# The first microseconds of a causal convolution and gated feed-forward kernel: softmax of the taps on eight partitions, the last band's products on ScalarE, and the first rows of x through SyncE's queue

## The chip, the cores and the metric

The kernel runs on one core of a Trainium2 chip. The core has TensorE (PE; matmuls, and PEld for its weight loads), VectorE (DVE), ScalarE (ACT), GpSimd (POOL) and SyncE (SP), each with its own instruction stream, and sixteen DMA engines which serve the transfers that SP, ACT and POOL issue. The metric is the device time of one execution in microseconds. Before the change three runs took 515.96, 516.28 and 517.74 us, with a median of 516.28 us.

## What is computed

The input x has 8 sequences of 3904 rows with 192 columns in fp32. The 192 columns belong to 8 heads of 24. For each head, a softmax over 7 weights gives 7 taps, and every row becomes the sum of itself and its six predecessors, weighted with the taps (a causal depthwise convolution, zero-padded at the start of a sequence). The 31232 resulting rows go through a gated feed-forward block.

```python
w = np.exp(weight - weight.max(-1, keepdims=True))
w = w / (w.sum(-1, keepdims=True) + 1e-09)          # 8 heads x 7 taps
x_pad = np.concatenate([np.zeros((B, 6, D)), x], axis=1)
out = np.einsum('hk,bskhg->bshg', w, x_unf)         # x_unf: rows s .. s+6 of x_pad, by heads
x = out.reshape(B * S, D)
a, b = x @ w1, x @ w2                               # 192 -> 1024
h = a * b @ w3                                      # 1024 -> 1024
return h @ w_out                                    # 1024 -> 192
```

## The kernel before

The tokens are split into two streams (NS = 2) of 15616 rows, r = 0 and r = 1. Partitions 0 to 63 hold stream 0 and partitions 64 to 127 stream 1, and a 64-row matmul works on one of them. w3 and w_out are multiplied with one another at the start (lines 550 to 570), so that in the steady part each round of 512 tokens per stream is two products: first_product (line 510; w1 and w2, cast by ScalarE, gated by VectorE) and second_product (line 520).

The convolution of the first batches is a matmul too. A window of x has 64 rows (Q), 58 of them new (ST) and 6 the predecessors (PAD). For each head a 64x64 "band" matrix holds the taps on its diagonals. conv (line 381) multiplies windows with bands, pe_transpose and joint_transposes (lines 445 and 596) turn the result for the products. Batches of windows are loaded by load_x(b) (line 112), from fp32 in memory to bf16 on the chip, on POOL's queue.

Instructions are in the program's order on every engine, and an engine waits at the head of its own stream. What happens in the first 16 us, in the order of the code:

- wall, the 8x7 weights, is loaded to one partition on ACT's queue (lines 143 and 144). VectorE sets constants (lines 157 to 163). ScalarE loads its table and does a first exponential (line 164).
- wfirst, the first quarter of w1 and w2 in fp32, is loaded by two DMAs on SP's queue (line 171).
- POOL issues load_x0(0), makes both halves of diag (line 183), issues load_x0(1), then two DMAs for the first window's 58 rows of each stream (line 189; the six rows before them are zeros, line 160), then load_x(1), load_w(1) (the second quarter of w1 and w2, already as bf16), casts one half of wfirst (cast_w(1, 1, ...), line 193), then load_w(2), load_x(2), and copies and loads on (lines 203 to 208).
- TensorE multiplies zeros for a while (warm(6), line 217).
- The softmax runs on one partition, 56 elements (lines 223 to 231): maximum, difference, exponential on ScalarE, sum, reciprocal, product. Two matmuls with the row `half` (line 237) spread the taps over 128 partitions, and they end in wsb.
- band(g, e) (line 252) makes c, the products of diag shifted by 7 taps with wsb, on VectorE, and 28 matmuls which add them up in PSUM; put (line 578) moves the result to Aband. There are four bands. ScalarE moves the first two, VectorE the other two, and ScalarE casts wfirst between and after them (lines 582 to 589).
- conv(0, 0, 4) and conv(0, 4, 4) follow (lines 622 and 623), three transposes, conv(1, 0, H), the first parts of the first product and, in the middle of the product of round 0 (line 652), conv(2, 0, 4) and conv(2, 4, 4), which read what load_x(2) brought.

There are four pairs of PSUM banks (banks and drained, lines 78 to 87); each step takes one pair and gives it back when its result has been moved.

Of the kernel before, what the change touches and what calls it, by code (L numbers as in the profile page):

```python
# [16 lines left out]
def kernel(  # L17
# [17 lines left out]
    PAD = K - 1  # L35

    NS = 2
    TS = B * S // NS
# [4 lines left out]
    Q = 64  # L43
    ST = Q - PAD
# [22 lines left out]
    const = ctx.enter_context(tc.tile_pool(name="const", bufs=1))  # L67
# [17 lines left out]
    def drained(p):  # L85
        assert p not in free
        free.append(p)
# [17 lines left out]
    x_rows = x.rearrange("b s d -> (b s) d")  # L105
    xb_of, zero_rows = {}, {}

    def x_spans(r, i, m):
        return bass.AP(tensor=x.tensor, offset=(r * TS + tok(i) - PAD) * D,
                       ap=[[D, Q], [ST * D, m], [1, D]])  # L110
# [29 lines left out]
            else:  # L140
                tiles.append((xb, 0))

    wall = const.tile([1, H, K], FP32)
    nc.scalar.dma_start(out=wall, in_=weight.rearrange("(o h) k -> o h k", o=1))
# [9 lines left out]
    half = const.tile([1, 3 * Q], BF16)  # L154
# [4 lines left out]
    nc.vector.memset(ones, 1.0)  # L159
    nc.vector.memset(xb0[:, 0, :], 0.0)  # L160
    nc.vector.memset(half, 0.0)
    nc.vector.memset(half[:, Q:2 * Q], 1.0)
    nc.vector.memset(ident, 0.0)
    nc.scalar.activation(out=tiny, in_=tiny, func=ACT.Exp)

    WC = (0, DFF // 4, DFF // 2, DFF * 3 // 4, DFF)
    wd = [const.tile([128, NP, DFF], BF16, name=f"wd{i}", tag=f"wd{i}") for i in range(2)]
    w_rows = [w.rearrange("(k q) f -> q k f", q=Q) for w in (moe_w1, moe_w2)]

    for i in range(2):  # L170
        nc.sync.dma_start(out=wfirst[:, i], in_=w_rows[i][:, :, 0:WC[1]])

    def load_w(part):
        cs = slice(WC[part], WC[part + 1])
        for i in range(2):
            nc.gpsimd.dma_start(out=wd[i][0:Q, :, cs], in_=w_rows[i][:, :, cs])  # L176

    def load_x0(r):
        nc.gpsimd.dma_start(out=xb0[Q * r:Q * r + Q, 1:, :], in_=x_spans(r, 1, 2 * n0 - 1))  # L179

    load_x0(0)
    for p0 in (0, Q):
        nc.gpsimd.affine_select(  # L183
            out=diag[p0:p0 + Q], in_=ones[p0:p0 + Q].to_broadcast([Q, Q + PAD]),
            pattern=[[-1, Q + PAD]], compare_op=ALU.is_equal, fill=0.0, base=0,
            channel_multiplier=1)
    load_x0(1)
    for r in range(NS):
        nc.gpsimd.dma_start(out=xb0[Q * r + PAD:Q * r + Q, 0, :],  # L189
                            in_=x_rows[r * TS:r * TS + ST, :])  # L190
    load_x(1)
    def cast_w(i, r, f):
        f(out=wd[i][Q * r:Q * r + Q, :, 0:WC[1]], in_=wfirst[:, i])  # L193
# [16 lines left out]
    def warm(n):  # L210
        p, t = banks()
        for j in range(n):
            nc.tensor.matmul(t[:, j % 2, :], zeros, zeros[:, 0:1].to_broadcast([128, CH]),
                             start=True, stop=True)
        drained(p)

    warm(6)

    wmax = const.tile([1, H], FP32)
    wsum = const.tile([1, H], FP32)  # L220
    wrow = const.tile([1, H, K], BF16)
    wsb = const.tile([128, 2, 2, K], BF16)
    nc.vector.reduce_max(out=wmax, in_=wall, axis=AX.X)
    nc.vector.tensor_tensor(
        out=wall, in0=wall, in1=wmax.unsqueeze(2).to_broadcast([1, H, K]), op=ALU.subtract)
    nc.scalar.activation(out=wall, in_=wall, func=ACT.Exp)
# [8 lines left out]
    wrow = wrow.rearrange("p (g e a) k -> p g e a k", g=2, a=2)  # L235
# [9 lines left out]
    def band_of(h, r):  # L245
# [3 lines left out]
    taps = bass.AP(tensor=d0.tensor, offset=d0.offset,  # L249
                   ap=[list(d0.ap[0]), [1, K], [1, Q]])  # L250

    def band(g, e):
        c = slot([128, K, Q], BF16, "cprod")
        nc.vector.tensor_tensor(
            out=c, in0=taps, in1=wsb[:, g, e].unsqueeze(2).to_broadcast([128, K, Q]),
            op=ALU.mult)
        p, bps = banks()
        for k in range(K):
            for v in range(2):
                for r in range(2):  # L260
                    rs = slice(Q * r, Q * r + Q)
                    o = Q * (r ^ v)
                    nc.tensor.matmul(bps[o:o + Q, v, 0:Q], ident[rs, rs], c[rs, k, :],
                                     start=(k == 0), stop=(k == K - 1))
        return p, Aband[:, g, e], bps[:, :, 0:Q]
# [115 lines left out]
    def conv(b, h0, nh, evict=None):  # L381
        n = SIZES[b] // 2
        if h0 == 0:
            tag, bufs = ("alone", 1) if GRID <= b else ("convo", 2)
            convo_of[b] = work.tile([128, n, NP, NS, Q], BF16, tag=tag, bufs=bufs, name="convo")
        convo = convo_of[b]
        p, cps = banks()
        wd = nh * G

        def view(ps, r):  # L390
            return cps[ps, r, 0:n * wd].rearrange("p (w g) -> p w g", g=wd)

        for j in range(nh):
            h = h0 + j
            for c in range(2):
                xb, w0 = xb_of[b][c]
                for r in range(NS):
                    nc.tensor.matmul(  # L398
                        view(slice(Q * c, Q * c + Q), r)[:, :, j * G:(j + 1) * G],
                        band_of(h, r),  # L400
                        xb[Q * r:Q * r + Q, w0:w0 + n, h * G:(h + 1) * G],
                        start=True, stop=True)
# [170 lines left out]
    V, A, P = nc.vector.tensor_copy, nc.scalar.copy, nc.gpsimd.tensor_copy  # L573
# [4 lines left out]
    def put(f, p, dst, src):  # L578
        f(out=dst, in_=src)
        drained(p)  # L580

    cast_w(0, 0, A)
    put(A, *band(0, 0))
    put(A, *band(0, 1))
    cast_w(0, 1, A)
    made = [band(1, 0), band(1, 1)]
    put(V, *made[0])
    put(V, *made[1])
    cast_w(1, 0, A)

    def move_all(p, moves, fs):
        for f, m in zip(fs, moves):
            move(f, m)
        drained(p)
# [92 lines left out]
    def put_rows(b, last):  # L687
# [7 lines left out]
        out=wv, in0=wv, in1=top.unsqueeze(2).to_broadcast([128, H, K]), op=ALU.subtract)  # L695
# [5 lines left out]
        out=wv, in0=wv, in1=top.unsqueeze(2).to_broadcast([128, H, K]), op=ALU.mult)  # L701
# [84 lines left out]
```

## Time and profile before

| | |
|---|---|
| median of three runs | 516.28 us |
| profiled execution | 517.34 us |
| its span, first to last instruction | 515.6 us |
| TensorE busy in the span | 508.2 us |
| VectorE busy | 401.9 us |
| ScalarE busy | 351.3 us |
| GpSimd busy | 321.4 us |
| granted TensorE clock | 1.000 |

All lines come from one profiled execution. A line of the timeline has the start in us from the beginning of the span, the length in us, the engine, the line of the code, the operation, the names out<-in, the shape, the number of instructions put together, and in brackets the idle time of the engine ahead of it with what ended that. An engine with a q behind its name (SPq, ACTq) is the issue of a DMA, not its transfer. A line of the waits has who waited for whom, us in total, times and the longest. In a group of instructions, the numbers behind the bar are busy us, mean ns of one, and the idle time before them; for one source line the numbers are the shortest, the median and the longest in ns, then the first and last start. In the DMA views q0 is the queue of the DMAs that POOL issues, q1 that of SP; a row has packets, MB, and the time that the packets took as a share of what sixteen DMA engines have in the window. Shares can exceed 100% since packets overlap on an engine. The windows rows have the length, the busy time of PE, PEld, DVE, ACT and POOL with the number of instructions, the granted clock, the DMA share and GB/s.

### The profile page before, as it was taken

The numbers are of one execution on the slowest core, as the hardware profiler recorded it, in microseconds if no ns is written. First come the engines' busy times: TensorE is split into PE (matmuls) and PEld (weight loads), VectorE is DVE, ScalarE is ACT, GpSimd is POOL, SyncE is SP. The second block draws the span as 40 slices with busy tenths as digits, with TensorE's granted clock in tenths as the row PEclk, the third lists the DMA queues.
The fourth block names the chain that finished last, engine by engine and source line by source line (L and its number), as shares of the span: only waits on it lengthen the run. The fifth ranks groups of instructions, "written<-read, shape, count | busy, mean of one in ns | idle before, by whom it ended". The sixth has DMA issues, their size and how long they took to land.

```text
span 515.6 us, 13632 instructions
## 1 busy us (share of the span) xinstructions
PE 508.2 (99%) x5608; PEld 338.9 (66%) x5608; DVE 401.9 (78%) x475; ACT 351.3 (68%) x466; POOL 321.4 (62%) x447
## 2 busy tenths in 40 slices
PE   8899999999999999999999999999999999999997
PEld 4444698555894558944589444884449855498577
DVE  6679723889958999589995999949999499972970
ACT  6787644777657776577765777657776577744762
POOL 8510624279999999899983999749997491000000
PEclk9999999999999999999999999999999999999999
DMA  9989999993984984787827798278932851025004
GB/s 119 165 153 123 145 194 204 195 208 80 134 251 130 131 104 101 241 156 100 103 83 240 147 106 98 93 239 140 108 46 93 247 122 32 1 99 174 7 3 154
DMA packets 137410, 67.91 MB, mean 132 GB/s; under 512 B 98899, under 2 KB 135939, under 8 KB 137283
## 3 DMA queue, kind: packets, MB, share of 16 engines
q0 software_dynamic: 48096, 26.92, 37.0%
q1 hardware_dynamic: 89105, 40.01, 33.5%
q8 instruction: 44, 0.72, 0.5%
q14 instruction: 19, 0.16, 0.1%
q10 hardware_dynamic: 146, 0.10, 0.1%
HBM read 39.60 MB, written 36.56 MB: 148 GB/s over the span
## 4 chain that ended last, share of the span: by engine, by line
PE 93%; DMA 3%; POOL 2%; ACT 1%; DVE 1%; issue 0%; POOLq 0%; ACTq 0%
PE pairs L481 58%; PE pairs L532 32%; PE pairs L398 2%; DMA xT<-rows 2%; DMA xb<-in_x_dram 1%; PE pairs L567 1%; ACT asb L489 1%; POOL wd L176 0%; DVE abT L500 0%; POOL xb L126 0%; PE pairs L606 0%; POOL xb L179 0%; POOL xb L189 0%; POOL wd L193 0%; POOL diag L183 0%
## 5 line engine op out<-in xcount | busy, mean ns | idle before, releaser
L500 DVE TENSOR_TENSOR abT<-asb,pairs 128x1024 bf16<-128x1024 bf16 (+1 forms) x245 | 298.0, 1217 | 70.1 <-ACT asb L489 53.6
L481 PE MATMUL pairs<-xT,wd 64*128 64x512 bf16 (+3 forms) x3000 | 319.7, 371 | 1.2 <-DMA xT<-rows 0.6
L489 ACT CAST asb<-pairs 128x1024 bf16<-128x1024 f32 (+1 forms) x245 | 247.1, 1009 | 68.1 <-PE pairs L481 68.0
L481 PEld LDWEIGHTS <-wd 64*128 64x128 bf16 x3000 | 160.2, 94 | 154.4 <-issue 2.9
L532 PE MATMUL pairs<-W_sb,abT 128*128 128x192 bf16 x1952 | 165.0, 246 | 0.0
L532 PEld LDWEIGHTS <-abT 128*128 128x128 bf16 x1952 | 159.9, 98 | 5.3 <-issue 5.1
L537 ACT COPY osb<-pairs 128x384 f32<-128x384 f32 x122 | 58.6, 480 | 83.3 <-PE pairs L532 82.6
L331 POOL TENSOR_TENSOR acc<-acc,term 128x384 f32<-128x384 f32 (+1 forms) x120 | 107.4, 895 | 9.4
L328 POOL TENSOR_TENSOR term<-xv,wv 128x384 f32<-128x384 bf16 (+1 forms) x144 | 107.6, 747 | 0.0
L317 DVE SCALAR_TENSOR_TENSOR pairs<-xv,wv,pairs 128x384 f32<-128x384 bf16 (+1 forms) x120 | 68.7, 572 | 7.2 <-ACT pairs L315 3.4
L364 POOL DMA_DIRECT2D rows<-y x6 | 3.7, 614 | 68.8 <-DVE y L320 59.9
L334 POOL TENSOR_TENSOR y<-acc,term 128x192 bf16<-128x192 f32 (+5 forms) x60 | 26.5, 467 | 1.9
L419 ACT CAST convo<-pairs 128x864 bf16<-128x864 f32 (+9 forms) x49 | 26.6, 615 | 1.6 <-PE pairs L398 1.5
L325 POOL TENSOR_TENSOR acc<-xv,wv 128x384 f32<-128x384 bf16 (+1 forms) x24 | 18.3, 763 | 12.5 <-DMA xv<-in_x_dram 12.4
L419 DVE CAST convo<-pairs 128x960 bf16<-128x960 f32 (+4 forms) x10 | 8.2, 858 | 17.2 <-PE pairs L398 17.2
L320 DVE SCALAR_TENSOR_TENSOR y<-xv,wv,pairs 128x192 bf16<-128x192 bf16 (+5 forms) x60 | 18.0, 351 | 1.1
L126 POOL DMA_DIRECT2D xb<-in_x_dram x20 | 13.9, 719 | 4.2 <-DMA xb<-in_x_dram 3.0
L342 POOL DMA_DIRECT2D xb<-in_x_dram x20 | 15.1, 772 | 0.0
L544 POOL DMA_DIRECT2D out_dram<-osb x8 | 6.1, 763 | 14.1 <-ACT osb L537 11.1
L398 PE MATMUL pairs<-xb,Aband 64*64 64x216 bf16 (+6 forms) x416 | 12.5, 238 | 1.5 <-DMA xb<-in_x_dram 1.4
L279 POOL DMA_DIRECT2D xv<-in_x_dram x12 | 13.0, 1088 | 0.0
L315 ACT ACTIVATE pairs<-xv,wv 128x384 f32<-128x384 bf16 (+1 forms) x24 | 12.8, 549 | 0.0
(65 smaller groups left out, 75.3 us busy)
## 6 DMA issues: line engine op xcount, KB each, us to landing
out_dram<-osb SPq DMA_DIRECT2D x52, 384.0 KB
xv<-in_x_dram POOLq DMA_DIRECT2D x10, 672.0 KB, 9.8
xb<-in_x_dram POOLq DMA_DIRECT2D x20, 216.0 KB, 7.8
rows<-y POOLq DMA_DIRECT2D x5, 768.0 KB, 5.5
out_dram<-osb POOLq DMA_DIRECT2D x8, 384.0 KB, 5.7
w3rows<-in_moe_w_dram POOLq DMA_DIRECT2D x2, 1024.0 KB, 11.8
xb<-in_x_dram POOLq DMA_DIRECT2D x8, 240.0 KB, 7.2
rows<-convo SPq DMA_DIRECT2D x6, 288.0 KB
```

Of the source, the lines that this page charges most:

```text
L317: f.scalar_tensor_tensor(out=flat, in0=xs(k), scalar=tap(k), in1=flat, op0=ALU.mult, op1=ALU.add)
L325: f.tensor_tensor(out=flat, in0=xs(PAD), in1=wide(PAD), op=ALU.mult)
L328: f.tensor_tensor(out=term.rearrange("p (m g) -> p m g", g=G), in0=xs(k), in1=wide(k), op=ALU.mult)
L331: f.tensor_tensor(out=acc, in0=acc, in1=term, op=ALU.add)
L334: f.tensor_tensor(out=dst, in0=by_row[:, :, r, cs], in1=term[:, :, r, cs], op=ALU.add)
L398: nc.tensor.matmul(view(slice(Q * c, Q * c + Q), r)[:, :, j * G:(j + 1) * G], band_of(h, r), xb[Q * r:Q * r + Q, w0:w0 + n, h * G:(h + 1) ...
L419: f[e % len(f)](out=dst, in_=part)
L481: nc.tensor.matmul(p[:, r, e * n:e * n + n], wd[i][rs, k, ft * 128:(ft + 1) * 128], xT[k][rs, r0 + c0:r0 + c1], start=(k == 0), stop=(k == ...
L489: nc.scalar.copy(out=asb, in_=pa)
L500: nc.vector.tensor_tensor(out=dst, in0=asb, in1=pb, op=ALU.mult)
L532: nc.tensor.matmul(ops[:, (g - g0) * D:(g - g0) * D + D], ab[:, jt, r, g * 128:(g + 1) * 128], W_sb[:, jt, :], start=(jt == 0), stop=(jt = ...
L537: f(out=osb[:, g0:g0 + per, :].rearrange("p g d -> p (g d)"), in_=ops[:, 0:per * D])
```

## The change

The weights are loaded to eight partitions, one head each, on SP's queue ahead of wfirst. The softmax is done with one head per partition: a negated maximum, an exponential with this maximum as bias, a sum, a reciprocal, and one instruction that multiplies with the reciprocal and with diag, so that each head's taps stand in its own block of columns and are zeros elsewhere. Two matmuls with a block of ones (8x64) spread them to the two halves of the partitions. The two copies of diag to ident go from VectorE to ScalarE. warm(6) becomes warm(5).

The bands are made in the order (0, 0), (0, 1), (1, 1), (1, 0). The products of (1, 1) are made by ScalarE, seven instructions of 128x64 with the taps from a copy wlast in fp32. VectorE moves the first two results, ScalarE the other two.

The 58 rows per stream of the first window are loaded as fp32 to a tile xfirst by two DMAs on SP's queue behind wfirst, and no longer by POOL to bf16. ScalarE casts them to xb0[:, 0, :] ahead of conv(0, ...). The second half of diag is made after load_x0(1). POOL casts both of wfirst's parts for partitions 64 to 127. ScalarE casts the parts for partitions 0 to 63 in halves: columns 0 to 127 of w1 ahead of conv(0, ...)'s evictions, those of w2 behind them, the rest after the three transposes.

```diff
-    wall = const.tile([1, H, K], FP32)
-    nc.scalar.dma_start(out=wall, in_=weight.rearrange("(o h) k -> o h k", o=1))
+    wall = const.tile([H, K], FP32)
+    nc.sync.dma_start(out=wall, in_=weight)
...
+    ones_h = const.tile([H, Q], BF16)
+    xfirst = const.tile([128, D], FP32)
...
-    nc.vector.memset(xb0[:, 0, :], 0.0)
-    nc.vector.memset(half, 0.0)
-    nc.vector.memset(half[:, Q:2 * Q], 1.0)
+    nc.vector.memset(xfirst, 0.0)
+    nc.vector.memset(ones_h, 1.0)
...
     for i in range(2):
         nc.sync.dma_start(out=wfirst[:, i], in_=w_rows[i][:, :, 0:WC[1]])
+    for r in range(NS):
+        nc.sync.dma_start(out=xfirst[Q * r + PAD:Q * r + Q, :],
+                          in_=x_rows[r * TS:r * TS + ST, :])
...
     load_x0(0)
-    for p0 in (0, Q):
...
+    diagonal(0)
     load_x0(1)
-    for r in range(NS):
-        nc.gpsimd.dma_start(out=xb0[Q * r + PAD:Q * r + Q, 0, :],
-                            in_=x_rows[r * TS:r * TS + ST, :])
+    diagonal(Q)
     load_x(1)
-    def cast_w(i, r, f):
-        f(out=wd[i][Q * r:Q * r + Q, :, 0:WC[1]], in_=wfirst[:, i])
+    def cast_w(i, r, f, c0=0, c1=WC[1]):
+        f(out=wd[i][Q * r:Q * r + Q, :, c0:c1], in_=wfirst[:, i, :, c0:c1])
...
     load_w(1)
-    cast_w(1, 1, nc.gpsimd.tensor_copy)
+    for i in range(2):
+        cast_w(i, 1, nc.gpsimd.tensor_copy)
...
-    warm(6)
+    warm(5)
...
-    wrow = const.tile([1, H, K], BF16)
+    wrow = const.tile([H, 2, 2, 2, K], BF16)
     wsb = const.tile([128, 2, 2, K], BF16)
-    nc.vector.reduce_max(out=wmax, in_=wall, axis=AX.X)
-    nc.vector.tensor_tensor(
-        out=wall, in0=wall, in1=wmax.unsqueeze(2).to_broadcast([1, H, K]), op=ALU.subtract)
-    nc.scalar.activation(out=wall, in_=wall, func=ACT.Exp)
-    nc.vector.tensor_copy(out=ident[0:Q, 0:Q], in_=diag[0:Q, 0:Q])
+    wlast = const.tile([128, K], FP32)
+    nc.vector.tensor_reduce(out=wmax, in_=wall, axis=AX.X, op=ALU.max, negate=True)
+    nc.scalar.activation(out=wall, in_=wall, func=ACT.Exp, bias=wmax)
+    nc.scalar.copy(out=ident[0:Q, 0:Q], in_=diag[0:Q, 0:Q])
     nc.vector.reduce_sum(out=wsum, in_=wall, axis=AX.X)
     nc.vector.reciprocal(out=wsum, in_=wsum)
-    nc.vector.tensor_tensor(
-        out=wrow, in0=wall, in1=wsum.unsqueeze(2).to_broadcast([1, H, K]), op=ALU.mult)
-    nc.vector.tensor_copy(out=ident[Q:128, Q:128], in_=diag[Q:128, 0:Q])
+    nc.vector.scalar_tensor_tensor(
+        out=wrow.rearrange("h g e a k -> h (g e a) k"),
+        in0=wall.unsqueeze(1).to_broadcast([H, H, K]), scalar=wsum,
+        in1=diag[0:H, 0:H].unsqueeze(2).to_broadcast([H, H, K]), op0=ALU.mult, op1=ALU.mult)
+    nc.scalar.copy(out=ident[Q:128, Q:128], in_=diag[Q:128, 0:Q])
...
     for a in range(2):
-        nc.tensor.matmul(wbc, half[:, Q - Q * a:Q - Q * a + 128], wrow[:, :, :, a],
-                         start=(a == 0), stop=(a == 1))
+        nc.tensor.matmul(wbc[Q * a:Q * a + Q], ones_h, wrow[:, :, :, a], start=True, stop=True)
     nc.vector.tensor_copy(out=wsb, in_=wbc)
+    nc.scalar.copy(out=wlast, in_=wbc[:, 1, 1])
...
         c = slot([128, K, Q], BF16, "cprod")
-        nc.vector.tensor_tensor(
-            out=c, in0=taps, in1=wsb[:, g, e].unsqueeze(2).to_broadcast([128, K, Q]),
-            op=ALU.mult)
+        if (g, e) == (1, 1):
+            for k in range(K):
+                nc.scalar.activation(out=c[:, k], in_=diag[:, k:k + Q], func=ACT.Copy,
+                                     scale=wlast[:, k:k + 1])
+        else:
+            nc.vector.tensor_tensor(
...
-    cast_w(0, 0, A)
-    put(A, *band(0, 0))
-    put(A, *band(0, 1))
-    cast_w(0, 1, A)
-    made = [band(1, 0), band(1, 1)]
-    put(V, *made[0])
-    put(V, *made[1])
-    cast_w(1, 0, A)
+    made = [band(0, 0), band(0, 1), band(1, 1), band(1, 0)]
+    for f, b in zip((V, V, A, A), made):
+        put(f, *b)
+    A(out=xb0[:, 0, :], in_=xfirst)
+    cast_w(0, 0, A, 0, 128)
...
     move_all(*conv(0, 4, 4, ()), (A, A))
+    cast_w(1, 0, A, 0, 128)
     for k, f in enumerate((V, V, A)):
...
         drained(p)
+    for i in range(2):
+        cast_w(i, 0, A, 128)
     move_all(*conv(1, 0, H, "streams"), (A, V))
```

More of the change, by code (lines that the diff above doesn't have):

```diff
@@ L153 @@
     zeros = const.tile([128, 128], BF16)
-    half = const.tile([1, 3 * Q], BF16)
+    ones_h = const.tile([H, Q], BF16)
+    xfirst = const.tile([128, D], FP32)
     ident = const.tile([128, 128], BF16)
@@ L179, in load_x0, with diagonal @@
         nc.gpsimd.dma_start(out=xb0[Q * r:Q * r + Q, 1:, :], in_=x_spans(r, 1, 2 * n0 - 1))
-    load_x0(0)
-    for p0 in (0, Q):
+    def diagonal(p0):
         nc.gpsimd.affine_select(
@@ L186 @@
             channel_multiplier=1)
+    load_x0(0)
+    diagonal(0)
     load_x0(1)
-    for r in range(NS):
-        nc.gpsimd.dma_start(out=xb0[Q * r + PAD:Q * r + Q, 0, :],
-                            in_=x_rows[r * TS:r * TS + ST, :])
+    diagonal(Q)
     load_x(1)
-    def cast_w(i, r, f):
-        f(out=wd[i][Q * r:Q * r + Q, :, 0:WC[1]], in_=wfirst[:, i])
+    def cast_w(i, r, f, c0=0, c1=WC[1]):
+        f(out=wd[i][Q * r:Q * r + Q, :, c0:c1], in_=wfirst[:, i, :, c0:c1])
     def copy_w(part, i, f):
@@ L215, in warm @@
         drained(p)
-    warm(6)
-    wmax = const.tile([1, H], FP32)
-    wsum = const.tile([1, H], FP32)
-    wrow = const.tile([1, H, K], BF16)
+    warm(5)
+    wmax = const.tile([H, 1], FP32)
+    wsum = const.tile([H, 1], FP32)
+    wrow = const.tile([H, 2, 2, 2, K], BF16)
     wsb = const.tile([128, 2, 2, K], BF16)
-    nc.vector.reduce_max(out=wmax, in_=wall, axis=AX.X)
-    nc.vector.tensor_tensor(
-        out=wall, in0=wall, in1=wmax.unsqueeze(2).to_broadcast([1, H, K]), op=ALU.subtract)
-    nc.scalar.activation(out=wall, in_=wall, func=ACT.Exp)
-    nc.vector.tensor_copy(out=ident[0:Q, 0:Q], in_=diag[0:Q, 0:Q])
+    wlast = const.tile([128, K], FP32)
+    nc.vector.tensor_reduce(out=wmax, in_=wall, axis=AX.X, op=ALU.max, negate=True)
+    nc.scalar.activation(out=wall, in_=wall, func=ACT.Exp, bias=wmax)
+    nc.scalar.copy(out=ident[0:Q, 0:Q], in_=diag[0:Q, 0:Q])
     nc.vector.reduce_sum(out=wsum, in_=wall, axis=AX.X)
     nc.vector.reciprocal(out=wsum, in_=wsum)
-    nc.vector.tensor_tensor(
-        out=wrow, in0=wall, in1=wsum.unsqueeze(2).to_broadcast([1, H, K]), op=ALU.mult)
-    nc.vector.tensor_copy(out=ident[Q:128, Q:128], in_=diag[Q:128, 0:Q])
+    nc.vector.scalar_tensor_tensor(
[3 more added lines that the diff above has]
+    nc.scalar.copy(out=ident[Q:128, Q:128], in_=diag[Q:128, 0:Q])
     pw, wbc = banks()
     wbc = wbc[:, 0, 0:H * K // 2].rearrange("p (g e k) -> p g e k", g=2, e=2)
-    wrow = wrow.rearrange("p (g e a) k -> p g e a k", g=2, a=2)
     for a in range(2):
-        nc.tensor.matmul(wbc, half[:, Q - Q * a:Q - Q * a + 128], wrow[:, :, :, a],
-                         start=(a == 0), stop=(a == 1))
+        nc.tensor.matmul(wbc[Q * a:Q * a + Q], ones_h, wrow[:, :, :, a], start=True, stop=True)
     nc.vector.tensor_copy(out=wsb, in_=wbc)
+    nc.scalar.copy(out=wlast, in_=wbc[:, 1, 1])
     drained(pw)
@@ L253, in band @@
         c = slot([128, K, Q], BF16, "cprod")
-        nc.vector.tensor_tensor(
-            out=c, in0=taps, in1=wsb[:, g, e].unsqueeze(2).to_broadcast([128, K, Q]),
-            op=ALU.mult)
+        if (g, e) == (1, 1):
[4 more added lines that the diff above has]
+            nc.vector.tensor_tensor(
+                out=c, in0=taps, in1=wsb[:, g, e].unsqueeze(2).to_broadcast([128, K, Q]),
+                op=ALU.mult)
         p, bps = banks()
```

## The prediction

> **What bounds the kernel now.** I read the page first, then TensorE's waits over the whole span, then the chain of waits and the timeline of the first 22 us.
>
> ```profile
> span 515.6 us, 13632 instructions
> PE 508.2 (99%) x5608; PEld 338.9 (66%) x5608; DVE 401.9 (78%) x475; ACT 351.3 (68%) x466; POOL 321.4 (62%) x447
> ```
>
> TensorE is busy in all but 7.4 us, so anything that moves its first dense stretch moves the end by as much. Its waits, longest first:
>
> ```profile
> PE pairs L398 <- DMA xb<-in_x_dram: 1.4, 1, 1.4
> PE pairs L213 <- DVE ones L159: 1.1, 1, 1.1
> PE pairs L481 <- DMA xT<-rows: 0.6, 1, 0.6
> ```
>
> The largest lies in the stretch that the change edits. The chain shows what ends it, and the timeline what TensorE does on both sides:
>
> ```profile
> 9.21 0.70 POOL xb L126
> 9.91 5.97 DMA xb<-in_x_dram
> ...
> 15.92 0.36 PE pairs L398 x15
> ```
>
> ```profile
> 0.81 0.51 ACTq L144 DMA_DIRECT2D wall<-in_weight_dram  x1
> 0.82 1.41 SPq L171 DMA_DIRECT2D wfirst<-in_moe_w_dram  x2
> ...
> 1.07 2.74 PE L213 MATMUL pairs<-zeros 128*128 128x512 bf16 x6 [1.07 <-DVE ones L159]
> ...
> 1.35 1.28 ACT L164 ACT_TABLE_LOAD   x1 [1.35 <-PEq L770]
> ...
> 2.11 0.20 DVE L223 TENSOR_REDUCE wmax<-wall 1x8 f32<-1x56 f32 x1 [0.62 <-DMA wall<-in_weight_dram]
> ...
> 2.76 0.23 ACT L226 ACTIVATE wall<-wall 1x56 f32<-1x56 f32 x1
> ...
> 3.52 1.10 POOL L189 DMA_DIRECT2D xb<-in_x_dram  x2
> ...
> 4.24 2.23 DVE L254 TENSOR_TENSOR cprod<-diag,wsb 128x448 bf16<-128x448 bf16 x4
> 4.47 0.83 ACT L193 CAST wd<-wfirst 64x768 bf16<-64x768 f32 x1 [1.49 <-DMA wfirst<-in_moe_w_dram]
> ...
> 4.91 2.20 PE L263 MATMUL pairs<-cprod,ident 64*64 64x64 bf16 x112
> 5.55 0.27 ACT L579 CAST Aband<-pairs 128x128 bf16<-128x128 f32 x1 [0.24 <-PE pairs L263]
> ...
> 6.90 0.86 PE L398 MATMUL pairs<-xb,Aband 64*64 64x72 bf16 x32
> ...
> 7.17 0.82 POOL L193 CAST wd<-wfirst 64x768 bf16<-64x768 f32 x1
> ...
> 14.33 0.23 PE L398 MATMUL pairs<-xb,Aband 64*64 64x96 bf16 x1
> ...
> 15.92 0.36 PE L398 MATMUL pairs<-xb,Aband 64*64 64x96 bf16 x15 [1.36 <-DMA xb<-in_x_dram]
> 16.21 1.47 PE L481 MATMUL pairs<-xT,wd 64*128 64x512 bf16 x12
> ```
>
> Read it as a race of two runners to 15.92, where conv(2, ...) goes on. One is TensorE's own front: bands, the first convolution at 6.90, transposes, first products, at conv(2, ...) at 14.33. The other is load_x(2), in only at 15.88. So the front has 1.6 us to spare: made shorter it gains nothing, made longer by more than that it delays everything.
>
> **The change, part by part.** *Softmax on eight partitions.* wall's DMA leaves ACT's queue (0.51 us ahead of the table load), so the load can end near 2.1 instead of 2.6; wall itself arrives as before (2.11); one DVE step is saved. The exponential runs at about 2.4 instead of 2.76, and the products start about 0.4 earlier, near 3.85. On SP, wall's issue (0.51) now stands ahead of wfirst, and everything on that queue is 0.5 later.
>
> *Last band by ScalarE.* DVE makes three products (0.56 each, 2.23/4): 3.85 to 5.5. ScalarE makes seven of 128x64. No row has that; bounds are the 56-column activation at 0.23 and this line's shortest, of 96 columns:
>
> ```profile
> L315 ACT ACTIVATE pairs<-xv,wv x24: 324/584/622, 132.2 to 462.7; 128x384 f32<-128x384 bf16 x20, 128x96 f32<-128x96 bf16 x4
> ```
>
> 1.6 to 2.3 us; I take 2.0 (0.28 each, between them), 3.9 to 5.9. TensorE's four bands (2.20/4 = 0.55 each) then end near 7.0, the last two evictions by ScalarE (0.27) near 7.2. That is as before, and it doesn't matter if the next part holds.
>
> *POOL.* Two issues (1.10) go, a cast (0.82) comes, ahead of load_x(2): issued about 0.28 earlier. The new cast waits for wfirst: in at 4.47, now about 5.0, POOL gets there near 6. Hidden.
>
> *The first stretches of x through SP.* This is the part that decides. Two DMAs of 58 rows by 768 B stand behind wfirst on SP's queue, plain fp32. How are so few, oddly many rows spread over the DMA engines? The nearest row is the one plain SP transfer here whose rows are no multiple of 16 and number more than 18: L359, 38 rows. Its issue, the next one's, and the DMA traffic in 342.15:342.40, before the next one's packets start:
>
> ```profile
> 340.02 1.38 SPq L359 DMA_DIRECT2D rows<-convo  x1
> 341.50 1.60 SPq L544 DMA_DIRECT2D out_dram<-osb  x2
> ```
>
> ```profile
> DMA packets 12, 0.01 MB, mean 31 GB/s; under 512 B 2, under 2 KB 12, under 8 KB 12
> ## 3 DMA queue, kind: packets, MB, share of 16 engines
> q1 hardware_dynamic: 12, 0.01, 12.4%
> ```
>
> 12.4% of sixteen engines is two engines, ten 768 B packets in 0.25 us: 50 ns each (0.25 x 2/10). So 38 rows went over two engines, 19 each. The bounds for 58 rows are two engines (29 each per DMA) and all sixteen (4 each). I take two, as the row has it, and the same two for both DMAs, since they are alike and on one queue: 58 packets each; different pairs (29 each) are the milder case below.
>
> In the Trainium skill, "DMA: Bandwidth & Descriptors", section "Why a DMA increments its semaphore by 16 and not by 1", the engine count of a SyncE or ScalarE transfer is the largest number up to 16 that divides the outer counts of both sides, and the lowest-numbered engines are used. By that rule 58 = 2 x 29 goes over two engines and both transfers share them; the 38-row transfer agrees with the count (12.4%), and no row shows which engines. It speaks against this edit, and by it the sum is the one that follows.
>
> Those packets share with POOL's. The traffic in 4.25:4.75, when both queues had work, then SP's last in 4.75:5.20, then 5.20:12.00:
>
> ```profile
> DMA packets 156, 0.11 MB, mean 226 GB/s; under 512 B 65, under 2 KB 156, under 8 KB 156
> ...
> q1 hardware_dynamic: 95, 0.09, 85.8%
> q0 software_dynamic: 61, 0.02, 33.4%
> ```
>
> ```profile
> q1 hardware_dynamic: 32, 0.02, 29.0%
> ```
>
> ```profile
> q0 software_dynamic: 2042, 0.82, 110.1%
> ```
>
> 156 packets in 0.5 us on sixteen engines are 51 ns each, 61% of them SP's. SP's queue (q1) is empty from 5.2 on, so wfirst drains by 5.1; 0.5 later now, 5.6 at worst. Then 58 packets at 51 ns and a 61% share: 58 x 0.051/0.61 = 4.85 us, from a start between 5.1 and 5.6, and 0.3 from the last packet to the semaphore, as for wall: its traffic in 0:2 stands in slice 36 of 40, at 1.8, and wmax starts at 2.11.
>
> ```profile
> GB/s 0 0 0 0 0 0 0 0 0 0 0 0 0 0 0 0 0 0 0 0 0 0 0 0 0 0 0 0 0 0 0 0 0 0 0 5 0 0 0 0
> ```
>
> That gives 10.25 to 10.75; I take 10.4. Bounds: alone on the engines, 5.1 + 58 x 0.050 + 0.3 = 8.3; half share and the late start, 5.6 + 5.9 + 0.3 = 11.8; sixteen engines, 5.6 + 8 x 0.051/0.61 + 0.3 = 6.6. Before, the same rows came through POOL 3.1 us after their issues at 3.5 and 4.1, just in time for 6.90:
>
> ```profile
> xb<-in_x_dram POOLq DMA_DIRECT2D x2, 21.8 KB, 3.1
> ```
>
> *The wait that this adds.* xb0[:, 0] = xfirst runs on ScalarE and needs both DMAs. Queued behind it there: half of cast_w(0, 0), conv(0, 4, 4)'s evictions, cast_w(1, 0), a transpose's move, asb; on TensorE all of conv(0, ...). The copy costs 0.31 (128x192 from PSUM, below) to 0.35. conv(0, ...) starts at 10.4 + 0.35 + 0.05 = 10.8 instead of 6.90.
>
> ```profile
> L576 ACT CAST convo<-pairs 128x192 bf16<-128x192 f32 x1 | 0.3, 307 | 0.0
> ```
>
> From there to conv(2, ...) it took 14.33 - 6.90 = 7.43. New in this stretch on ScalarE are four half casts, about 0.5 each (0.83 has 768 columns and some 0.2 fixed, so 384 cost 0.51). Two lie beside TensorE's convolutions and transposes, where before the tail of a whole cast lay; two (1.0) stand between the transposes' move and conv(1, ...)'s, which the first asb follows. Of these I count 0.7 on the path; bounds 0 and 1.2. Arrival: 10.8 + 7.43 + 0.7 = 18.9.
>
> *The other runner.* On the two engines load_x(2) stands behind 58 packets more and about 8 fewer: 50 x 0.051 = 2.6 later at most, 15.88 + 2.6 - 0.28 = 18.2. That is before 18.9, hidden. The sum: 18.9 - 15.92 = **3.0 us later**, and from 16 on nothing gives it back, as TensorE is dense.
>
> The profiled execution took 517.34 (span 515.6 and 1.7 around it), 1.06 above the median of three, 516.28. It would become 520.3; against the median I forecast **519.3**.
>
> **The rivals.**
>
> *The clock falls as well (slower still).* TensorE would idle from 7.0 to 10.8. Its first six 512-column matmuls took 2.74/6 = 0.46 each, while later twelve half-array ones, two at a time, took 1.47/6 = 0.245 a pair: the array starts at about half speed. If the idle time puts it back, the next 3.4 us run at half speed (the slow stretch at the start lasted from 1.07 to at least 4 us; I take 3.4). TensorE is busy in most of this stretch:
>
> ```profile
> 6.90:14.33 7.43, 6.76 (x154) 4.27 (x147) 5.33 (x12) 5.61 (x11) 7.39 (x12) 1.00 1.16 133
> ```
>
> So up to 1.7 lost, less slack 0.7: about 1.4 on top, 520.7. Against it: the wait before 15.92 didn't slow the matmuls at 16.21; but it was 1.4 us, not 3.8. The Trainium skill, "TensorE: Matmul & The Clock Gate", section "Part 1: The HAM clock gate", lets an idle window of about 3.4 us halve the clock; with a free-running window 3.8 us of idling need not hold a whole one. No stretch of this trace tests it.
>
> *The rows come sooner, but late (about level).* Different pairs of engines, or POOL's packets mostly giving way: landed near 8.4, conv(0, ...) at 8.8, arrival 16.9, **+1.0**, 517.3.
>
> *Not slower: the rows are spread and hidden.* With sixteen engines xfirst is in at 6.6, before ScalarE has put the last band (7.2). conv(0, ...) starts near 7.6, arrives at 7.6 + 7.43 + 0.7 = 15.7, and load_x(2), 0.28 earlier, is in at 15.6. The front's slack absorbs it all: -0.2, 516.1. For it: the same rows through POOL cost no visible wait. Against it: the 38-row transfer. It decides if xfirst lands before about 7.2.
>
> *Faster.* The whole wait at conv(2, ...) is 1.36 and the front would have to shrink as well, to win 1.6: 514.7. Nothing here shortens load_x(2) by that.
>
> **How the numbers follow.** Late rows with the clock kept 0.50 (519.3); with the clock down 0.20 (520.7); milder 0.13 (517.3); hidden 0.11 (516.1); faster 0.06 (514.7). 0.3% of 516.28 is 1.55 us, about what a measurement of this kernel can tell. The first two and a good half of the milder case lie above 517.83: slower 0.78, within 0.16, faster 0.06. The range goes from 517.0, just under the milder case, to 521.2, which is the clock case with the rows in at 10.9; the latest landing (11.8) with the clock down would be beyond it, hidden and faster below it.
>
> **What would show it.** Right: ScalarE's copy of xfirst waits on its DMA, for some 3 us, and starts near 10.4; TensorE's largest wait moves to conv(0, ...), and the one at conv(2, ...) is gone or short; q1 goes on to about 10 at two engines' share. Wrong: xfirst in before 7.5 with conv(2, ...) waiting until about 15.7 (spread); matmuls after the wait at twice their length (clock); the first asb less than 0.4 later after conv(0, ...) than before (half casts hidden).

## The result and the profile after

| | before | after |
|---|---|---|
| median | 516.39 us (515.69 to 517.74, 6 runs) | 519.31 us (518.34 to 520.37, 6 runs) |
| profiled execution | 517.34 us | 520.37 us |
| its span | 515.6 us | 518.7 us |
| granted TensorE clock | 1.000 | 0.993 |

The ratio is 1.0058, with a 95% interval from 1.0036 to 1.008: the changed kernel is slower by some 3 us, and the forecast was 519.3. The page of the changed kernel:

```profile
span 518.7 us, 13644 instructions
PE 509.0 (98%) x5607; PEld 338.3 (65%) x5607; DVE 400.4 (77%) x470; ACT 353.1 (68%) x478; POOL 321.2 (62%) x446
```

TensorE was idle for 9.7 us of its span instead of 7.4. Its longest waits:

```profile
PE pairs L407 <- ACT xb L594: 3.5, 1, 3.5
PE pairs L217 <- DVE ones L160: 1.1, 1, 1.1
PE pairs L490 <- DMA xT<-rows: 1.0, 1, 1.0
```

The wait for load_x(2) at conv(2, ...) is gone, and conv(0, ...) (L407) waits 3.5 us for ScalarE's copy of xfirst. What the copy waited for stands in the chain of the changed kernel:

```profile
3.18 6.33 DMA xfirst<-in_x_dram
...
9.60 0.36 ACT xb L594
```

The transfer ends at 3.18 + 6.33 = 9.51. The same stretch in the timeline of the changed kernel:

```profile
4.04 1.70 DVE L263 TENSOR_TENSOR cprod<-diag,wsb 128x448 bf16<-128x448 bf16 x3
4.16 1.78 ACT L260 ACTIVATE cprod<-diag,wlast 128x64 bf16<-128x64 bf16 x7
...
4.71 1.76 PE L272 MATMUL pairs<-cprod,ident 64*64 64x64 bf16 x112
...
6.31 0.52 ACT L588 CAST Aband<-pairs 128x128 bf16<-128x128 f32 x2 [0.37 <-PE pairs L272]
...
8.93 1.40 POOL L126 DMA_DIRECT2D xb<-in_x_dram  x2
9.60 0.35 ACT L594 CAST xb<-xfirst 128x192 bf16<-128x192 f32 x1 [2.76 <-DMA xfirst<-in_x_dram]
...
10.00 0.70 PE L407 MATMUL pairs<-xb,Aband 64*64 64x72 bf16 x32 [3.52 <-ACT xb L594]
...
12.76 1.92 PE L490 MATMUL pairs<-xT,wd 64*128 64x348 bf16 x12
...
18.97 0.36 PE L407 MATMUL pairs<-xb,Aband 64*64 64x96 bf16 x16
```

The bands were ready by 6.83, before the old start of conv(0, ...), 6.90. conv(0, ...) started at 10.00, 3.10 later, and conv(2, ...) was reached at 18.97 instead of 15.92, 3.05 later. The span is 3.1 longer.

Between the two points something else happened. Twelve half-array matmuls of the first product took 1.92 us, and in the kernel before 1.06. The windows of the changed kernel show why:

```profile
9.00:10.00 1.00, 0.00 (x1) 0.00 (x1) 0.00 (x0) 0.41 (x2) 1.00 (x2) 0.77 0.94 110
10.00:12.00 2.00, 1.58 (x41) 1.34 (x40) 1.10 (x3) 1.46 (x4) 1.53 (x3) 0.50 1.19 135
12.00:14.00 2.00, 2.00 (x45) 1.19 (x44) 0.95 (x3) 1.70 (x5) 2.00 (x4) 0.50 1.16 133
14.00:16.00 2.00, 2.00 (x18) 0.96 (x16) 1.21 (x3) 0.94 (x2) 2.00 (x4) 0.50 0.75 100
16.00:18.00 2.00, 2.00 (x38) 1.45 (x36) 0.81 (x2) 1.37 (x2) 2.00 (x4) 0.91 0.56 53
```

By these rows the clock was granted at half for nearly 7 us, from about 9.5, still within TensorE's wait, to about 16.4. From conv(0, ...) to conv(2, ...) it took 8.97 us instead of 7.43 (14.33 - 6.90 in the kernel before).

### The profile page after: what moved, and what is told of

The parts are those of the page before. It is cut to its first block, busy times and chain, and to the rows that moved or that the text cites. A ratio compares the mean times of both kernels' runs of the same rounds, so it can differ in the third digit from the quotient of the medians.

```text
span 518.7 us, 13644 instructions
## 1 busy us (share of the span) xinstructions
PE 509.0 (98%) x5607; PEld 338.3 (65%) x5607; DVE 400.4 (77%) x470; ACT 353.1 (68%) x478; POOL 321.2 (62%) x446
## 4 chain that ended last, share of the span: by engine, by line
PE 94%; DMA 3%; ACT 1%; DVE 1%; issue 0%; SPq 0%; ACTq 0%
PE pairs L490 59%; PE pairs L541 32%; PE pairs L407 2%; DMA xT<-rows 2%; DMA xfirst<-in_x_dram 1%; PE pairs L576 1%; ACT asb L498 1%; DVE abT L509 0%; PE pairs L612 0%; DMA wall<-in_weight_dram 0%; PE pairs L460 0%; DVE convo L585 0%; ACT xb L594 0%; ACT osb L546 0%; ACT wall L229 0%
## 5 line engine op out<-in xcount | busy, mean ns | idle before, releaser
L334 POOL TENSOR_TENSOR acc<-xv,wv 128x384 f32<-128x384 bf16 (+1 forms) x24 | 18.3, 764 | 11.2 <-DMA xv<-in_x_dram 11.1
L407 PE MATMUL pairs<-xb,Aband 64*64 64x216 bf16 (+6 forms) x416 | 12.4, 245 | 3.5 <-ACT xb L594 3.5
L407 PEld LDWEIGHTS <-Aband 64*64 64x64 bf16 x416 | 7.9, 113 | 8.7 <-issue 8.7
```

Of the source, the lines that this page charges most:

```text
L334: f.tensor_tensor(out=flat, in0=xs(PAD), in1=wide(PAD), op=ALU.mult)
L407: nc.tensor.matmul(view(slice(Q * c, Q * c + Q), r)[:, :, j * G:(j + 1) * G], band_of(h, r), xb[Q * r:Q * r + Q, w0:w0 + n, h * G:(h + 1) ...
```

## The experiments

The question was how the 3.05 us divide between the transfer's engines, its place on the queue, the clock and the parts that touch the softmax and the bands. Each kernel was timed beside the kernel before. Arrivals are the starts of conv(0, ...) and conv(2, ...) in the kernel's own profiled execution.

| kernel | median us | before us | ratio (95% interval) | conv(0) | conv(2) |
|---|---|---|---|---|---|
| the kernel before | | | | 6.90 | 15.92 |
| the change, first series | 519.31 | 516.39 | 1.0058 (1.0036 to 1.008) | 10.00 | 18.97 |
| g4_after_again: the change | 518.80 | 516.37 | 1.0035 (1.0019 to 1.0051) | 9.72 | 18.73 |
| e1_split: xfirst cut in 48 + 10 rows | 518.01 | 516.48 | 1.0032 (1.0017 to 1.0047) | 8.64 | 17.73 |
| e4_bridge: TensorE kept busy | 518.18 | 516.48 | 1.0038 (1.0026 to 1.0051) | 9.59 | 17.33 |
| g1_split_bridge: both | 516.63 | 516.37 | 0.9998 (0.9982 to 1.0015) | 8.53 | 16.28 |
| e3_alone: before, xfirst moved | 517.93 | 516.48 | 1.0028 (1.0015 to 1.0042) | 8.70 | 17.70 |
| e2_pool: rows back on POOL's queue | 517.14 | 516.48 | 1.0016 (1.0002 to 1.0030) | 7.70 | 16.03 |
| g3_pool_wall_act: and wall on ACT's | 517.02 | 516.37 | 1.0005 (0.9987 to 1.0022) | 6.89 | 16.04 |
| h2_split_wall_act: cut, wall on ACT's | 516.78 | 516.58 | 1.0012 (1.0002 to 1.0022) | 8.15 | 16.51 |
| h1_split_first: cut, ahead of wfirst | 517.39 | 516.58 | 1.0026 (1.0012 to 1.0040) | 7.10 | 16.62 |
| g2_swap_before: before, load_x(2) earlier | 516.64 (11 runs; a twelfth took 523.20) | 516.37 | 1.0005 (0.9980 to 1.0030) | 6.88 | 14.61 |
| h3_pool_act_swap: g3, load_x(2) earlier | 517.88 | 516.58 | 1.0028 (1.0004 to 1.0052) | 6.85 | 14.96 |

The ratios are estimates of their own with their intervals, not the quotients of the medians beside them. Where the two differ, by up to 0.12% (0.6 us), the size of an effect in time is known no better; the arrivals are sharper.

### The same kernel again

> The changed kernel itself, beside these others on one chip: a second profile and the base for the bridge's gain. Expected ratio 1.005 to 1.0065; xfirst in at 9.1 to 9.6; clock at 0.5 from about 9 to 16 if the fall is no accident of the first profile.

The loss came again, with 2.43 us between the medians against 2.92 in the first series; the ratio, 1.0035, is below what was expected. xfirst landed at 9.24, the copy waited 2.54 us, and the clock was at half once more: its mean was 0.993 in all twelve runs. This is the base for the next three kernels.

### Two engines, or sixteen

```diff
     for r in range(NS):
-        nc.sync.dma_start(out=xfirst[Q * r + PAD:Q * r + Q, :],
-                          in_=x_rows[r * TS:r * TS + ST, :])
+        for s0, s1 in ((0, 48), (48, ST)):
+            nc.sync.dma_start(out=xfirst[Q * r + PAD + s0:Q * r + PAD + s1, :],
+                              in_=x_rows[r * TS + s0:r * TS + s1, :])
```

> The changed kernel with each 58-row transfer of xfirst cut in two, of 48 and 10 rows, on the same queue at the same place. Theory (58 rows run on two DMA engines, and this alone makes the loss): xfirst is in at 6.3 to 6.9 us, ScalarE's copy waits under 0.3 us or not at all, conv(0, ...) starts at 7.1 to 7.5, and conv(2, ...) is held by load_x(2) again, at 15.3 to 15.9; median 515.6 to 516.6, level with the kernel before. Rival A (the transfer is late because it stands behind wall and wfirst, whatever its cut): xfirst in after 8.0, 518 or more. Rival B (ScalarE's new work, the half casts and the last band's products, makes more than half of the loss): conv(0, ...) after 8.0 or conv(2, ...) not before 17, 517.5 or more.

The DMA view of the changed kernel from 5.4 to 9.1 us:

```profile
q0 software_dynamic: 1119, 0.45, 101.3%
q1 hardware_dynamic: 148, 0.11, 12.1%
```

SP's queue (q1) held 12.1% of sixteen engines in these 3.7 us; two engines would be 12.5%. The end of wfirst is in it (148 packets, and the rows are 116): from 5.9 to 9.1 the share is 9.5%, more than one engine and less than two. That fits both 58-row transfers on the same two engines, which have POOL's packets to carry as well. In e1_split, from 5.4 to 7.7:

```profile
q0 software_dynamic: 908, 0.34, 123.8%
q1 hardware_dynamic: 189, 0.11, 24.4%
```

Its packets were through by 7.3 (from 7.3 to 8.2 the queue has none). The copy and the convolutions of e1_split in the timeline:

```profile
8.23 0.35 ACT L595 CAST xb<-xfirst 128x192 bf16<-128x192 f32 x1 [1.45 <-DMA xfirst<-in_x_dram]
...
8.64 0.69 PE L408 MATMUL pairs<-xb,Aband 64*64 64x72 bf16 x32 [2.20 <-ACT xb L595]
...
17.73 0.36 PE L408 MATMUL pairs<-xb,Aband 64*64 64x96 bf16 x16
```

The cut brought the copy 1.09 us forward (9.32 in the repeated run, 8.23 here) and conv(2, ...) 1.00. In time the medians show 0.8 us, but the intervals of the two ratios overlap almost wholly. So the two engines are a cause of the late rows, but not the whole: 6.3 to 6.9 was expected for the landing, and that missed. The signs of both rivals came in (landing after 8.0, a median of 518 or more), and the kernels below tell them apart. The trace of e1_split shows two more things. Spread over more engines, SP's packets had to share with POOL's: in the window above they took 24.4% of sixteen engines and POOL's 123.8%. And about 0.9 us passed between the last packets (7.2) and the landing, which the chain of e1_split puts at 4.09 + 4.04 = 8.13; in the changed kernel it was 0.4 (9.1 and 9.51). What fills this time was not found.

### The clock

```diff
     A(out=xb0[:, 0, :], in_=xfirst)
+    warm(12)
```

> The changed kernel with twelve matmuls of zeros on TensorE between the bands and conv(0, ...), where it idles for 3.5 us. xfirst is as late as before (9.4 to 9.6), so the start of conv(0, ...) stays at 10.0. Theory: if the fallen clock costs what I priced (1.4, in the profiled run of the change 8.97 instead of 8.13 from conv(0, ...) to conv(2, ...), 0.84), the clock stays up, conv(2, ...) comes at 18.0 to 18.3, and the median falls by 0.5 to 0.9, to 518.4 to 518.8. Rival: the clock's fall is hidden behind ScalarE and VectorE, nothing changes (519.0 to 519.6). A delay of conv(0, ...) beyond 10.2 would say that twelve are too many.

These are twelve matmuls of zeros whose results nobody reads (the trace has eleven of them). They fill TensorE's wait. The timeline of e4_bridge, then its windows:

```profile
6.38 2.79 PE L217 MATMUL pairs<-zeros 128*128 128x512 bf16 x11
...
9.59 0.45 PE L407 MATMUL pairs<-xb,Aband 64*64 64x72 bf16 x32 [0.42 <-ACT xb L595]
...
11.72 1.06 PE L490 MATMUL pairs<-xT,wd 64*128 64x348 bf16 x12
13.16 0.51 PE L613 MATMUL pairs<-ident,convo 128*128 128x128 bf16 x6 [0.38 <-ACT convo L585]
...
17.33 0.36 PE L407 MATMUL pairs<-xb,Aband 64*64 64x96 bf16 x16
```

```profile
10.00:12.00 2.00, 1.45 (x51) 1.09 (x47) 1.44 (x5) 1.64 (x5) 1.77 (x3) 1.00 1.13 120
```

conv(0, ...) starts about as late as in the changed kernel, for xfirst is as late. But the clock stays whole, the twelve matmuls take 1.06 again, and conv(0, ...) to conv(2, ...) takes 7.74 instead of 8.97 to 9.01: **the clock is worth 1.25 us of the arrival**, more than the 0.84 expected (conv(2, ...) at 18.0 to 18.3). In time this kernel alone doesn't show it: the medians are 0.6 apart (518.80 and 518.18), the ratios 1.0035 and 1.0038. With the rows cut as well, and eight such matmuls, it does:

> Both repairs together: xfirst cut in 48 and 10 rows, and eight matmuls of zeros between the bands and conv(0, ...). With the cut alone the rows were in at 8.2, conv(0, ...) ran at 8.64 and, at half clock, conv(2, ...) at 17.73. Theory now (three causes: two engines 1.4 us, the place in SP's queue, and a clock that falls while TensorE waits, 1.3 us): conv(0, ...) at 8.5 to 8.9, clock 1.00 from 10 to 16, conv(2, ...) at 16.2 to 16.7; ratio to the kernel before 1.0005 to 1.0015, that is 0.8 less than with the cut alone. Rival (the clock's fall is part of how these runs look, but the time goes elsewhere): no less than 1.0027.

g1_split_bridge, timeline:

```profile
8.13 0.35 ACT L596 CAST xb<-xfirst 128x192 bf16<-128x192 f32 x1 [1.36 <-DMA xfirst<-in_x_dram]
...
8.53 0.45 PE L408 MATMUL pairs<-xb,Aband 64*64 64x72 bf16 x32 [0.27 <-ACT xb L596]
...
16.28 0.36 PE L408 MATMUL pairs<-xb,Aband 64*64 64x96 bf16 x16
```

Of the 2.8 us at conv(2, ...) in the repeated run (18.73), 0.36 is left, and the time is level with before. Against e1_split, whose copy starts within 0.1 us of this one, only the matmuls of zeros differ: conv(2, ...) comes 1.45 earlier, the distance of the medians to before falls from 1.53 to 0.26, and the intervals no longer overlap (1.0017 to 1.0047 there, 0.9982 to 1.0015 here). That a wait filled with useless work wins time shows the clock's part.

### The move alone, and the rest alone

e3_alone is the kernel before with nothing changed but xfirst: the two transfers go through SP's queue behind wfirst, and ScalarE copies.

> The kernel before with this one part of the change alone: xfirst by two 58-row transfers behind wfirst on SP's queue, cast by ScalarE right ahead of conv(0, ...), POOL's two issues gone. wall stays on ACT's queue, so SP's queue is some 0.5 us earlier than in the changed kernel, and no half casts stand behind conv(0, ...). Theory: xfirst in at 8.8 to 9.4, conv(0, ...) at 9.2 to 9.9, conv(2, ...) some 7.4 later (8.3 if the clock falls), 16.6 to 18.2; 517.2 to 518.6, the greater part of the loss. Rival A as for the theory. Rival B: 516.9 or less, under a quarter of the loss.

```profile
8.30 0.35 ACT L591 CAST xb<-xfirst 128x192 bf16<-128x192 f32 x1 [0.42 <-DMA xfirst<-in_x_dram]
...
8.70 0.76 PE L399 MATMUL pairs<-xb,Aband 64*64 64x72 bf16 x32 [1.77 <-ACT xb L591]
...
17.70 0.36 PE L399 MATMUL pairs<-xb,Aband 64*64 64x96 bf16 x16
```

The move alone, in the timeline of e3_alone, brings the late copy, half the clock (9.00 us between the two convolutions), 1.78 us at conv(2, ...) and 1.45 us of the median. The rows came earlier than expected (landing at 8.22, not 8.8 to 9.4). e2_pool is its opposite: the changed kernel with these rows back on POOL's queue, as bf16, and without the copy.

> The changed kernel with this one part undone: the 58 rows of each stream come through POOL's queue as bf16, ahead of load_x(1), and the copy of xfirst goes. Theory: conv(0, ...) starts at 6.6 to 7.3, conv(2, ...) goes on at 15.7 to 16.3 (two issues, 1.1 us, and two casts now stand ahead of load_x(2)); 516.0 to 517.0. Rival B (ScalarE's new work): 517.5 or more.

```profile
7.70 0.57 PE L406 MATMUL pairs<-xb,Aband 64*64 64x72 bf16 x32 [1.25 <-DMA xb<-in_x_dram]
...
16.03 0.36 PE L406 MATMUL pairs<-xb,Aband 64*64 64x96 bf16 x16
```

In this timeline of e2_pool the bands end early and conv(0, ...) waits 1.25 us for POOL's rows, 0.8 later than before and 0.4 later than expected. They were in just in time before. g3_pool_wall_act puts wall's load back on ACT's queue as well:

> The changed kernel with two parts undone: the 58 rows through POOL's queue as bf16, and wall's DMA on ACT's queue again (still 8x7). With the first alone, the same POOL issues as in the kernel before (3.5 and 4.1) landed at 7.8 instead of 7.0. Theory: that was wall's issue ahead of wfirst on SP's queue (0.46 us), which lays wfirst's packets over these rows; undone, the rows are in at 6.9 to 7.2, conv(0, ...) at 7.1 to 7.4, and load_x(2), issued 0.75 later than before, holds conv(2, ...) until 15.8 to 16.4; ratio 0.9995 to 1.001. Rival (POOL's or ScalarE's order makes it): rows in at 7.6 or later, ratio 1.0015 or more.

```profile
6.89 0.87 PE L406 MATMUL pairs<-xb,Aband 64*64 64x72 bf16 x32
...
14.88 0.23 PE L406 MATMUL pairs<-xb,Aband 64*64 64x96 bf16 x1
16.04 0.36 PE L406 MATMUL pairs<-xb,Aband 64*64 64x96 bf16 x15 [0.93 <-DMA xb<-in_x_dram]
```

conv(0, ...) is back at its old place without a wait, so wall's place held up POOL's rows (that wfirst's later packets then met theirs on the engines is likely, but wasn't shown), conv(2, ...) waits for load_x(2) as before, and the time is level. So the softmax on eight partitions, ScalarE's band and the half casts cost no time that can be measured, and bring none either. They are not free: TensorE reaches conv(2, ...) at 14.88 here and at 14.33 before, and the wait for load_x(2) hides these 0.55 us.

### The place on the queue

h2_split_wall_act is e1_split with wall's DMA issued by ScalarE; h1_split_first is e1_split with the four xfirst DMAs ahead of wfirst's two.

> The changed kernel with xfirst cut into 48 and 10 rows per stream and wall's DMA back on ScalarE's queue. Theory, wall's issue ahead of wfirst and xfirst on SyncE's queue costs some 0.5 to 0.8 us: xfirst is in at 7.3 to 7.7 (8.15 with the cut alone), conv(0) at 7.8 to 8.2, the idle time of TensorE before it under 1.5 us; conv(2) at 15.6 to 16.0 if the clock stays up, 17.0 if it falls. Ratio 0.9995 to 1.002. Rival, wall's place is nothing here: conv(0) at 8.6 again, ratio 1.003.

> The changed kernel with xfirst cut into 48 and 10 rows per stream and its four DMAs ahead of wfirst's two on SyncE's queue. Theory, the place on the queue matters: with wall's issue (0.4 us) and four issues of 0.44 us, xfirst is in by about 5.0 us, ScalarE's copy waits for nothing, conv(0) starts when the bands are moved and the rows cast, near 7.0 (8.64 with the rows cut but behind wfirst), and the clock stays up. wfirst is issued 1.75 us later, in near 7.8, GpSimd's casts end about 1.2 us later and load_x(2) is in near 17.0: conv(2) waits for it until about 16.7, 0.8 later than in the kernel before (ratio 1.001 to 1.003). Rival, the engines' sharing with GpSimd's packets decides and not the order on the queue: xfirst in at 7.5 or later, conv(0) after 8.0.

The timeline of h2_split_wall_act, then that of h1_split_first:

```profile
8.15 0.69 PE L408 MATMUL pairs<-xb,Aband 64*64 64x72 bf16 x32 [1.08 <-ACT xb L595]
...
10.91 1.92 PE L491 MATMUL pairs<-xT,wd 64*128 64x348 bf16 x12
...
16.51 0.36 PE L408 MATMUL pairs<-xb,Aband 64*64 64x96 bf16 x16
```

```profile
7.10 0.74 PE L408 MATMUL pairs<-xb,Aband 64*64 64x72 bf16 x32 [0.65 <-ACT xb L595]
...
7.23 0.82 POOL L197 CAST wd<-wfirst 64x768 bf16<-64x768 f32 x1 [1.25 <-DMA wfirst<-in_moe_w_dram]
...
16.62 0.36 PE L408 MATMUL pairs<-xb,Aband 64*64 64x96 bf16 x15 [0.81 <-DMA xb<-in_x_dram]
```

Each step forward on SP's queue brings conv(0, ...) forward: 8.64 behind wall and wfirst, 8.15 behind wfirst alone, 7.10 behind wall alone, where the copy waits for no transfer. The rival, sharing with POOL's packets whatever the order, falls. But ahead of wfirst it only hands the lateness on. POOL's casts wait for wfirst, load_x(2) stands behind them on POOL's queue, and conv(2, ...) waits 0.81 us for it, at 16.62. That the clock of h1_split_first would stay up was expected, and it didn't: it was at half from about 9.2 to 12.6. h2_split_wall_act is the better of the two, still 0.59 us late at conv(2, ...).

### An earlier load_x(2)

If the front has 1.6 us to spare, load_x(2) ahead of load_w(2) on POOL's queue should turn that into time, in the kernel before and in g3_pool_wall_act:

```diff
-    load_w(2)
     load_x(2)
+    load_w(2)
```

> The kernel before with one exchange on POOL's queue: load_x(2) ahead of load_w(2). It tests the second runner: that the kernel before is held at 15.92 by load_x(2) alone. Theory: load_x(2) is issued at 7.9 instead of 9.2 and has 768 packets fewer ahead of it, in at 13.0 to 14.2; conv(2, ...) runs through from 14.3, nothing later waits for load_w(2); 1.2 to 1.6 us less, ratio 0.9969 to 0.9977. Rival (DMA-bound whatever the order, or the late load_w(2) is waited for): ratio 0.999 or more.

> The changed kernel with the first rows back on GpSimd's queue, wall back on ScalarE's queue, and load_x(2) ahead of load_w(2). Theory, the softmax and band parts leave a front that can use an earlier load_x(2): conv(2) at 14.9 without the wait of 0.93 us, 1.0 us earlier than in the kernel before, ratio 0.998 if the start's gain is kept to the end. Rival, as with the same swap in the kernel before, what the front wins is given back in later waits for transposed rows (TensorE waiting for the DMA of xT, 1.8 us there): ratio 1.000 within 0.002.

conv(2, ...) came at 14.61 and 14.96 without a wait, 1.3 and 1.0 us earlier than before. Neither kernel is faster; h3_pool_act_swap is even 0.28% slower by its ratio, which its own profiled execution (span 515.3 against 515.6) doesn't show and no run explains. The gain is gone by about 112 us, behind waits of TensorE for the transposed rows of x. g2_swap_before has three of them, 1.8 us in all, where the kernel before has the one of 0.6:

```profile
PE pairs L481 <- DMA xT<-rows: 1.8, 3, 1.2
```

The last of them in the kernel before, g2_swap_before and h3_pool_act_swap, in this order, from their timelines:

```profile
111.33 20.46 PE L481 MATMUL pairs<-xT,wd 64*128 64x512 bf16 x188 [0.62 <-DMA xT<-rows]
```

```profile
111.91 20.46 PE L481 MATMUL pairs<-xT,wd 64*128 64x512 bf16 x188 [1.18 <-DMA xT<-rows]
```

```profile
111.13 20.46 PE L489 MATMUL pairs<-xT,wd 64*128 64x512 bf16 x188 [0.74 <-DMA xT<-rows]
```

TensorE waited longer here than before, and went on 0.58 us later and 0.20 us earlier: nothing is left of the first gain, and little of the second. Most of it had gone ahead of this wait, which g2_swap_before reached at 110.73 (111.91 - 1.18), the kernel before at 110.71 and h3_pool_act_swap at 110.39. The same wait stands in the profiled execution of the change:

```profile
114.61 20.46 PE L490 MATMUL pairs<-xT,wd 64*128 64x512 bf16 x188 [0.99 <-DMA xT<-rows]
```

It is in none of the other nine profiled executions, the repeated run of the change among them. That run's span is 517.3 where this one's is 518.7: of the 1.4 us between them, 0.24 is there at conv(2, ...) and 0.99 is this wait. So in one and the same kernel it comes and goes, and it may be behind part of the spread of the runs (514.72 to 520.44 in the eleven of g2_swap_before). What sets it was not found.

## Why the prediction was right, and which of its steps were not

The time was right (519.3 forecast, 519.31 measured), and so was the deciding mechanism. That the time came out so exactly is luck: three terms of the sum were off by 0.4 to 1.2 us, in opposite directions, and the same kernel measured again was at 518.80.

- *58 rows over two engines, and both transfers over the same two*: right as far as the traffic shows: 12.1% of sixteen engines, and the cut gained 1.09 us.
- *58 packets at 51 ns and a 61% share, landing at 10.4*: too late by 0.9. 58 packets on each engine took the 3.7 us from 5.4 to 9.1, 64 ns each, where 84 was forecast, and xfirst was in at 9.51. The value lay inside the bounds (8.3 to 11.8). The share had been read off while wfirst's packets and POOL's were spread over all engines; it didn't carry over to a queue that has work on two.
- *The copy, 0.35 + 0.05, and conv(0, ...) right behind it*: right, 9.60 to 10.00. The start was 10.00 and not 10.8.
- *"Late rows with the clock kept"*, the likeliest case with 0.50: the step that failed. The clock fell, as in the first rival, which had 0.20. The rival's mechanism is what happened, and its size too: 1.4 us was forecast on top, and 1.23 to 1.27 was measured (8.97 and 9.01 against 7.74). What spoke against it, a wait of 1.4 us that hadn't slowed the matmuls behind it, was no evidence: e2_pool lost half its clock after waits of 1.25 and 0.53.
- *Half casts, 0.7 on the path*: too high. With the clock kept the whole stretch took 0.31 more (7.74 in e4_bridge against 7.43), within the bounds of 0 and 1.2. TensorE waits 0.38 there (at 13.16) for a move of ScalarE's that stands behind two of the half casts. But no run takes the half casts out alone: g2_swap_before, without them, took 7.73, and at half clock e3_alone, without them, took 9.00 against 8.97 and 9.01. Their own share isn't shown.
- *Arrival 18.9 = 10.8 + 7.43 + 0.7*: it came at 18.97 = 10.00 + 7.43 + 0.31 + 1.23. Landing and half casts were 1.2 too high together, and the missing clock made up for it.
- *load_x(2) 0.28 earlier on POOL, and hidden*: right. It was issued at 8.93 instead of 9.20, and the wait at conv(2, ...) is gone.
- *The softmax and the bands end as before and don't matter*: right. The products started 0.2 earlier, not 0.4 (4.04 against 4.24), the bands were moved by 6.83 (7.2 forecast), and with the rows back on POOL's queue and wall on ACT's the time was level (1.0005, 0.9987 to 1.0022).
- *wall's issue delays everything on SP's queue by 0.5*: right in size (8.64 to 8.15 in conv(0, ...)), but the sum let it act on wfirst and xfirst only. In e2_pool it also held up POOL's rows by 0.8.
- *From 16 on nothing gives it back*: right for a loss, for in every kernel with a later conv(2, ...) the median follows this arrival within 0.6 us. For a gain it doesn't hold, as the two swaps show.

## What to carry to other kernels

Before a small load moves to another queue, ask over how many DMA engines its shape is spread and what stands ahead of it there; a load of 58 rows on two engines behind two loads of weights came 3 us too late, and cutting it into 48 and 10 rows brought it 1.09 us forward, at the price of two more transfers. A new wait of TensorE near the start has a second price beside its length, the clock behind it: look at the time of a known group of matmuls after the wait, and if the wait can't be removed, fill it with matmuls of zeros. A front made faster gained nothing here, since later waits took it back within 100 us: look for them before counting a gain.

## What the runs showed of the hardware

The clock fell after short waits. TensorE waited 3.5, 2.20 and 1.25 us ahead of conv(0, ...) in the changed kernel, e1_split and e2_pool. In the first two the clock was at half for nearly 7 us. In e2_pool it fell behind a second wait, of 0.53 us from 8.27, and was at half for about 3.4, from 8.8 to 12.2, as its windows show:

```profile
8.00:9.00 1.00, 0.47 (x34) 0.35 (x22) 0.81 (x2) 0.66 (x3) 1.00 (x2) 0.91 0.97 119
9.00:10.00 1.00, 1.00 (x17) 0.71 (x19) 0.60 (x3) 0.45 (x3) 1.00 (x3) 0.50 0.20 24
...
12.00:13.00 1.00, 1.00 (x14) 0.55 (x12) 0.53 (x1) 0.44 (x2) 1.00 (x3) 0.89 1.04 102
```

In h1_split_first waits of 0.65 and 0.53 us were enough, but a single one of 1.36 us left the clock whole in the kernel before (12 matmuls in 1.47 us behind it). So the length of one wait doesn't decide, and what does was not found.

The shorter spell costs less: 8.33 us from conv(0, ...) to conv(2, ...) in e2_pool, 7.74 with the clock kept, 8.97 to 9.09 with the longer spell. The Trainium skill, "TensorE: Matmul & The Clock Gate", section "Part 1: The HAM clock gate", gives the return to the half clock after at least one idle window of about 3.4 us. The runs here agree with steps of about 3.4 us in how long it lasts, but no wait of 3.4 us was needed for the fall; the measurement decides.

The recorded clock can miss such a spell. For h2_split_wall_act it was 1.00 in every window from 4 to 16 us, though the twelve matmuls at 10.91 took 1.92 us, as long as in the changed kernel at half. The durations are the better witness.
